# First layer by seven products, mixed with the second layer of the group before, and attention by whole chunks

## The chip, the cores and the metric

The kernel runs on one core of a Trainium2 chip. The metric is the time of one execution on the device in microseconds; the median over the runs is compared. Engines are named as in the profile: PE (TensorE; PEld are its weight loads), DVE (VectorE), ACT (ScalarE), POOL (GpSimd) and SP (SyncE, which here only issues DMAs).

## The reference

Two stages follow each other. The first is a linear attention with decay: 4 batches, 8 heads, 768 positions, 64 channels per head, computed in blocks with a state per head.

```python
intra = einsum('bhic,bhjc->bhij', qb, kb) * Dmask[None]      # lam ** (i - j), zero above the diagonal
intra = einsum('bhij,bhjd->bhid', intra, vb)
inter = einsum('bhid,bhde->bhie', qb * lam_pow[None], kv_state)
out[:, :, sl] = intra + inter
kv_state = lam_block * kv_state + einsum('bhsd,bhse->bhde', kb * rev_pow[None], vb)
```

Its result, as 3072 tokens of 512 numbers, goes through two dense layers: h = x @ w_in (512 to 2048), g = h * tanh(softplus(h)), out = g @ w_out (2048 to 512). Inputs and output are float32; the kernel computes in float16 with float32 sums.

## The kernel before, in words

Chunks have 128 positions; six groups n = 0 to 5 hold the four batches' chunks n, 512 tokens each. Per chunk the eight heads are four pairs of 64 + 64 channels. A dense first layer of a group (`mm1_unit`, L420) is 16 units of 4 matmuls with 512 columns, each followed by one Mish on ACT (L434). The second layer is plain for group 0 (`mm2_unit`, L442: 16 steps of 4 matmuls with 512 columns). For groups 1 to 5 it is Strassen's scheme in Winograd's form (`fast_unit`, L525): seven products of 2 x 8 matmuls with 256 columns, with sums of weights (`tsum`, L479) and of tokens (`gsum`, L498) made on DVE, and the results put together by `after`.

Attention works by half chunks (four heads). `att_a` scales q by its decay on DVE (`qT`, L318) and copies the scaled k into a zero-padded tile `kz` (L322); `att_s` makes scores from them with padded, full-height matmuls (L358) and masks them on DVE (`sb`, L362); `att_o` adds the state's part and the scores' part (L375, L379); the state is updated by `raw` on DVE (L298) and `w` on POOL (L299). k is scaled on POOL (`scale_k`, L259, on DVE for the first and last group). Group 0 has a form of its own, `first_t`, `first_s`, `first_o`: raw scores from half-height matmuls (L230), which are multiplied by a full table of decays `dm` (L234).

The order of work is written out by hand: each engine runs its instructions in the program's order. Group n's two layers run one after the other on PE, and the pieces of attention of group n + 1 are spread over them by a table (`room`). k, q and v come in chunk by chunk, 128 KB each in float16, by DMAs that POOL issues (L69, L77, L80); the weights come by POOL too (L93, L96, L103). Transposes of q and k from group 2 on are DMAs on SP. [...]

## Time and profile before

| what | value |
|---|---|
| median of 3 runs | 220.56 us (219.73 to 220.97) |
| profiled execution | span 217.4 us; the page gives no other time of it |
| median less that span | 3.2 us |
| granted clock of TensorE | 1.000 |
| loads by POOL's queue | 13.37 MB written, 78,080 packets |

The page gives busy time and share of the span for each engine; the chain of waits goes back from the last instruction to what released it at each step. In rows of the timeline the columns are start, length, engine, line, operation, tiles, count and, in brackets, how long the engine was idle before and what ended that. In the table by stage, behind each engine's busy time stands the number of its instructions, then the clock, the DMA engines' share and GB/s.

### The profile page before, as it was taken

How to read it: one execution, taken by the hardware profiler on the slowest of the kernel's cores; microseconds unless marked ns; L12 is line 12 of the kernel's file. 1: busy time of each engine (PE TensorE's matmuls, PEld its weight loads, DVE VectorE, ACT ScalarE, POOL GpSimd, SP SyncE). 2: the span in 40 equal slices, each digit the busy share in tenths (PEclk: the TensorE clock that was granted, in tenths of full speed). 3: DMA queues.
4: the chain of work that ended last, by engine and by line, in shares of the span. 5: the costliest groups of instructions: out<-in, count | busy, mean ns of one | idle time of the engine just before them, and what ended most of it. 6: DMA issues, size and time to landing. Idle time of an engine off the chain costs nothing.

```text
span 217.4 us, 4272 instructions
## 1 busy us (share of the span) xinstructions
PE 204.8 (94%) x1672; PEld 136.6 (63%) x1672; DVE 146.1 (67%) x309; ACT 101.3 (47%) x190; POOL 116.6 (54%) x139
## 2 busy tenths in 40 slices
PE   7899999999999799999979999979999999999993
PEld 2465544576545587745669845669845699644893
DVE  6667561877669999339999419999439987213433
ACT  5465566567665231166522176623166632266410
POOL 7996334998988768808757908757700002000020
PEclk9999999999999999999999999999999999999999
DMA  9999999999999999975999965999985201300014
...
DMA packets 103766, 24.66 MB, mean 113 GB/s; under 512 B 93890, under 2 KB 103234, under 8 KB 103746
## 3 DMA queue, kind: packets, MB, share of 16 engines
q0 software_dynamic: 78080, 13.37, 80.3%
...
q8 instruction: 13, 0.21, 0.4%
...
## 4 chain that ended last, share of the span: by engine, by line
PE 63%; DVE 20%; POOL 5%; issue 4%; DMA 4%; ACT 1%; ACTq 0%; POOLq 0%; DVEq 0%
PE ph L420 26%; PE z L525 10%; PE po L442 6%; PE y L525 6%; PE x L525 5%; DVE qT L318 5%; DVE kz L322 4%; DVE sb L362 4%; DVE gsum L498 4%; DMA win<-in_moe_w_in_dram 4%; PE pO L379 3%; DVE raw L298 3%; PE pS L358 2%; PE fin L525 2%; POOL vz L80 2%
## 5 line engine op out<-in xcount | busy, mean ns | idle before, releaser
L420 PE MATMUL ph<-xt,win 128*128 128x512 f16 (+2 forms) x404 | 89.6, 368 | 0.5 <-ACT hsg L434 0.2
L434 ACT ACTIVATE hsg<-ph 128x512 f16<-128x512 f32 x96 | 57.0, 597 | 45.6 <-PE ph L420 45.5
L420 PEld LDWEIGHTS <-win 128*128 128x128 f16 x404 | 37.0, 98 | 35.1 <-issue 0.6
L299 POOL TENSOR_TENSOR w<-raw,lbm 128x256 f16<-128x256 f32 x32 | 25.2, 791 | 29.0 <-DVE raw L298 28.9
L578 POOL TENSOR_TENSOR u<-u,p 128x512 f32<-128x512 f32 x5 | 6.5, 1293 | 52.0 <-DVE u L576 52.0
L525 PEld LDWEIGHTS <-gsum 128*128 128x128 f16 x336 | 30.8, 98 | 3.5 <-issue 0.5
L362 DVE TENSOR_TENSOR sb<-pS,maskT 128x512 f16<-128x512 f32 x40 | 27.2, 683 | 2.0 <-PE pS L358 1.9
L382 ACT ACTIVATE xt<-pO 128x256 f16<-128x256 f32 x40 | 15.2, 382 | 27.4 <-PE pO L379 27.2
L318 DVE TENSOR_TENSOR qT<-qraw,lq 128x256 f16<-128x256 f16 x32 | 19.1, 598 | 10.3 <-DMA qraw<-qn 10.3
L525 PEld LDWEIGHTS <-hsg 128*128 128x128 f16 x240 | 22.7, 98 | 2.5
L69 POOL DMA_DIRECT2D kn<-in_k_dram x23 | 21.4, 932 | 4.5 <-DMA win<-in_moe_w_in_dram 1.7
...
L498 DVE TENSOR_TENSOR gsum<-hsg 128x1024 f16<-128x1024 f16 x20 | 14.5, 725 | 12.9 <-ACT hsg L434 12.9
L322 DVE COPY kz<-kraw 64x256 f16<-64x256 f16 x64 | 19.9, 311 | 1.9 <-DMA kraw<-ktil 0.9
L379 PE MATMUL pO<-sb,vz 128*128 128x128 f16 x160 | 17.3, 219 | 3.6 <-DVE sb L362 3.2
L525 PE MATMUL z<-tsum,gsum 128*128 128x256 f16 x160 | 20.4, 272 | 0.2
L525 PE MATMUL x<-wout,hsg 128*128 128x256 f16 x160 | 20.1, 273 | 0.0
L358 PE MATMUL pS<-qT,kz 128*128 128x128 f16 x160 | 16.6, 220 | 1.8 <-DVE kz L322 1.6
L358 PEld LDWEIGHTS <-kz 128*128 128x128 f16 x160 | 11.8, 98 | 7.8 <-DVE kz L322 3.0
L298 DVE TENSOR_TENSOR raw<-pv,w 128x256 f32<-128x256 f32 x32 | 13.5, 422 | 4.1 <-PE pv L283 3.4
L379 PEld LDWEIGHTS <-vz 128*128 128x128 f16 x160 | 12.6, 98 | 5.7 <-issue 4.9
...
## 6 DMA issues: line engine op xcount, KB each, us to landing
...
win<-in_moe_w_in_dram POOLq DMA_DIRECT2D x3, 512.0 KB, 10.1
...
```

The costliest lines, as they stand in the source:

```text
L69: nc.gpsimd.dma_start(out=kn[i], in_=chunk_rows(k, i))
L80: nc.gpsimd.dma_start(out=vz[i % NVB][:, :, 0:D], in_=chunk_rows(v, i))
L299: nc.gpsimd.tensor_tensor(out=w_new, in0=raw, in1=lb, op=ALU.mult)
L318: nc.vector.tensor_tensor(out=s.qT, in0=qraw[i][:, 2 * hf : 2 * hf + 2, :], in1=lqh, op=ALU.mult)
L322: nc.vector.tensor_copy(s.kz[rs, :, hp, :], kraw[i][rs, 2 * hf : 2 * hf + 2, :])
L358: nc.tensor.matmul(psS[:, 2 * p + hp, :], s.kz[:, p, hp, :], s.qT[:, p, :], start=True, stop=True,)
L362: nc.vector.tensor_tensor(out=s.sb, in0=psS, in1=bc(maskT, 1, 4), op=ALU.mult)
L379: nc.tensor.matmul(psO[:, p, :], vf[:, o : o + 128], s.sb[:, 2 * p + hp, :], start=False, stop=(hp == 1))
L420: nc.tensor.matmul(ph_t[ni][:, lo:hi], win0[min(ni, 2)][:, kc, max(ni - 2, 0) * 128 : max(ni - 2, 0) * 128 + 128] if ni < w else win[ni // ...
L434: nc.scalar.activation(hsg[n][:, ni, :], ph_t.pop(ni), AF.Mish)
L498: nc.vector.tensor_tensor(out=gsum[n, i][:, ks, :], in0=a, in1=b, op=op)
L525: nc.tensor.matmul(t, lhs(kk, b), rhs(kk, c, c + w), start=(fresh and kk == 0 and (alone or i == 0)), stop=(kk == HK - 1), skip_group_chec ...
```

## The change

The first layer gets the same seven-product scheme as the second: a "set" is a quarter of its output rows (512 of 2048), seven products of 4 matmuls with 256 columns (`seven`, `set_step`), with sums of weights (`wsum`) and of tokens (`xsum`) from DVE. Groups 2 to 5 take it for all four sets, group 1 for two of them; group 0 keeps plain units. Group 0's second layer takes the seven products too (`dense2`). The loop over n now mixes three things, product by product: group n's second layer, group n + 1's first layer and group n + 2's attention (`quarter`: one set, three or four halves of second-layer products, one chunk). Group 1's attention stands among group 0's units. Attention runs by whole chunks in the form that group 0 had: raw scores from half-height matmuls in banks e and o, `dm` on DVE, and q decayed on the side for the state's part (`qd`). `kz`, its copies and the mask go. Loads are pairs of chunks (256 KB), and the first two groups' pairs stand between the weights' pieces. Each PSUM bank has one tag and one buffer: A, B, C for sets and units, G, H for the second layer, e, o, z for attention. `raw` has one buffer, the state's `w` one per batch.

```diff
+    def bank(tag, shape, dtype=F32):
+        return ps.tile([128] + shape, dtype, name=f"b{tag}", tag=f"b{tag}")
...
+    def load_pair(t, n, bp):
+        src, store = {"k": (k, kn), "q": (q, qn), "v": (v, vn)}[t]
+        if t == "v":
+            tile_ = vz[(2 * n + bp) % NVP]
+            nc.gpsimd.dma_start(out=tile_[:, :, 0:D], in_=rows(v, n, 2 * bp, 2))
+        else:
+            tile_ = loads.tile([128, 2 * H, D], F16, name=f"{t}n", tag=f"{t}n", bufs=4)
+            nc.gpsimd.dma_start(out=tile_, in_=rows(src, n, 2 * bp, 2))
+        pairs[t, n, bp] = tile_
+        for i in range(2):
+            store[n, 2 * bp + i] = tile_[:, i * H : (i + 1) * H, :]
...
+    load_win(0, 256, WQ)
+    load_win(1)
+    for t in "kqv":
+        load_pair(t, 1, 0)
+    load_win(2)
+    load_win(3)
+    for t in "kqv":
+        load_pair(t, 1, 1)
     for s in range(WS):
         load_wout(s)
...
+    def scores(n, b):
+        p_ = [bank(t, [JP, C]) for t in "eo"]
         for j in range(JP):
             for t in range(2):
                 rs = slice(64 * t, 64 * t + 64)
...
+                nc.tensor.matmul(p_[t][:, j, :], kT[n, b][rs, j, :], qT[n, b][rs, j, :],
+                                 start=True, stop=True)
         for t in range(2):
...
+            sb[n, b, t] = work.tile([128, JP, C], F16, name="sb", tag="sb", bufs=4)
+            nc.vector.tensor_tensor(out=sb[n, b, t], in0=p_[t], in1=dm[:, t], op=ALU.mult)
+    def outputs(n, b, tag="z"):
+        po = bank(tag, [JP, C])
+        vf = vn[n, b].rearrange("p h c -> p (h c)")
+        if n > 0:
+            for j in range(JP):
+                nc.tensor.matmul(po[:, j, :], wst[n, b][:, j, :], qd[n, b][:, j, :],
+                                 start=(j == 0), stop=False, skip_group_check=True)
         for j in range(JP):
             for t in range(2):
                 o = 4 * D * j + D * t
...
+                nc.tensor.matmul(po[:, j, :], vf[:, o : o + 128], sb[n, b, t][:, j, :],
+                                 start=(n == 0 and j == 0 and t == 0), stop=(t == 1),
+                                 skip_group_check=True)
+        nc.scalar.activation(x_tile(n)[:, :, b * C : (b + 1) * C], po, AF.Copy)
+    def state(n, b, tag="e"):
+        pv = bank(tag, [JP, 128])
+        for j in range(JP):
...
+                pv[:, j, :].rearrange("p (a e) -> p a e", a=2), flat(kd[n, b], j),
+                vn[n, b][:, 2 * j : 2 * j + 2, 0:D], start=True, stop=True)
+        w_new = const.tile([128, JP, 128], F16, name=f"w{b}") if n == 0 else wst[n, b]
         if n == 0:
...
+            nc.vector.tensor_tensor(out=w_new, in0=pv, in1=lbm, op=ALU.mult)
...
+            raw = work.tile([128, JP, 128], F32, name="raw", tag="raw", bufs=1)
+            nc.vector.tensor_tensor(out=raw, in0=pv, in1=wst[n, b], op=ALU.add)
+            nc.gpsimd.tensor_tensor(out=w_new, in0=raw, in1=lbm, op=ALU.mult)
+        wst[n + 1, b] = w_new
...
+    def w_sum(s, i, eng):
+        w, t = win[s], wsum[s]
+        a, b_, op = (
+            (w[:, 0:2, HC:], w[:, 2:4, HC:], ALU.add),
+            (t[:, 0], w[:, 0:2, 0:HC], ALU.subtract),
+            (w[:, 0:2, 0:HC], w[:, 0:2, HC:], ALU.subtract),
+            (w[:, 2:4, 0:HC], t[:, 1], ALU.subtract),
+        )[i]
+        eng.tensor_tensor(out=t[:, i], in0=a, in1=b_, op=op)
...
+    def x_sums(n):
+        x = xt[n]
+        t = [work.tile([128, 2, HC], F16, name=f"xsum{i}", tag=f"xsum{i}", bufs=1) for i in range(4)]
+        xsum[n] = t
+        for i, (a, b_) in enumerate((
+            (x[:, 0:2, HC:], x[:, 0:2, 0:HC]),
+            (x[:, 2:4, HC:], t[0]),
+            (x[:, 2:4, HC:], x[:, 0:2, HC:]),
+            (x[:, 2:4, 0:HC], t[1]),
+        )):
+            nc.vector.tensor_tensor(out=t[i], in0=a, in1=b_, op=ALU.subtract)
...
+    def seven(o, i, t, fresh):
+        w, x, ws, xs = win[o.s], xt[o.n], wsum[o.s], xsum[o.n]
+        for u in range(2):
+            for kk in range(2):
+                us = slice(u * 128, u * 128 + 128)
...
+                nc.tensor.matmul(t[:, u, :], lhs, rhs, start=(fresh and u == 0 and kk == 0),
+                                 stop=(kk == 1), skip_group_check=True)
...
+    def set_step(o, step):
+        if step == "m1":
+            o.a = bank("A", [2, HC])
+            seven(o, 1, o.a, True)
+            o.b = bank("B", [2, HC])
+            nc.scalar.activation(o.b, o.a, AF.Copy)
+        elif step == "m5":
+            o.c = bank("C", [2, HC])
+            seven(o, 5, o.c, True)
+            o.p5 = work.tile([128, 2, HC], F32, name="p5", tag="p5", bufs=1)
+            nc.scalar.activation(o.p5, o.c, AF.Copy)
+        elif step == "m2":
+            seven(o, 2, o.a, False)
+            mish(o, 0, 0, o.a)
+        elif step == "m6":
+            seven(o, 6, o.b, False)
+            nc.vector.tensor_tensor(out=o.c, in0=o.b, in1=o.p5, op=ALU.add)
+        elif step == "m7":
+            seven(o, 7, o.b, False)
+            c22 = work.tile([128, 2, HC], F32, name="c22", tag="c22", bufs=1)
+            nc.vector.tensor_tensor(out=c22, in0=o.b, in1=o.p5, op=ALU.add)
+            mish(o, 1, 1, c22)
+        elif step == "m3":
+            seven(o, 3, o.c, False)
+            mish(o, 0, 1, o.c)
+        elif step == "m4":
+            seven(o, 4, o.b, False)
+            mish(o, 1, 0, o.b)
...
+            if p == 1:
+                m.h = bank("H", [2, HN])
+                nc.scalar.activation(m.h, m.g, AF.Copy)
+            elif p == 2:
+                o = osum()
+                nc.scalar.activation(o, m.g, AF.Copy)
+                store(n, 0, 0, o)
+            elif p == 5:
+                m.p5 = work.tile([128, 2, HN], F32, name="r5", tag="r5", bufs=1)
+                nc.scalar.activation(m.p5, m.g, AF.Copy)
+                m.u4 = work.tile([128, 2, HN], F32, name="u4", tag="u4", bufs=1)
+                nc.vector.tensor_tensor(out=m.u4, in0=m.h, in1=m.p5, op=ALU.add)
+            elif p == 7:
+                o = osum()
+                nc.vector.tensor_tensor(out=o, in0=m.h, in1=m.p5, op=ALU.add)
+                store(n, 1, 1, o)
+            elif p == 3:
+                o = osum()
+                nc.vector.tensor_tensor(out=o, in0=m.g, in1=m.u4, op=ALU.add)
+                store(n, 0, 1, o)
...
+    state(0, 3, "o")
+    for i in range(2, NVP):
+        nc.vector.memset(vz[i][:, :, D : 2 * D], 0.0)
+    for bp in range(2):
+        for t in "kqv":
+            load_pair(t, 2, bp)
+    next_unit()
+    turn1(0)
+    next_unit()
+    decay_k(1, 0, nc.vector)
+    next_unit()
+    scores(1, 0)
+    turn1(1)
...
+    next_unit()
+    turn1(2)
+    next_unit()
+    decay_k(1, 2, nc.vector)
+    outputs(1, 1)
+    state(1, 1)
+    scores(1, 2)
...
+    next_unit()
+    w_sum(1, 0, nc.vector)
+    for ni, tag in ((0, "A"), (1, "B"), (2, "C")):
+        unit_part(1, ni, tag, 0, HC, True)
+    outputs(1, 3)
+    state(1, 3)
+    turn_dma(2, 0)
...
+    for part in range(2):
+        for i in (2, 0, 1, 3):
+            token_sum(0, i, part)
+    for ni in range(3):
+        unit_part(1, ni, "", HC, GT, False)
+        unit_end(1, ni)
+    unit(1, 3, "A")
+    for i in range(2):
+        weight_sum(0, i)
+        weight_sum(1, i)
+    for ni, tag in ((8, "B"), (9, "C"), (10, "A"), (11, "B")):
+        unit(1, ni, tag)
+    for i in range(2):
+        weight_sum(2, i)
+        weight_sum(3, i)
+    x_sums(1)
+    for i in range(1, 4):
+        w_sum(1, i, nc.vector)
...
+        set_step(o, "m1")
+        if att:
+            decay_q(m, b)
+        if n > 0:
+            if qi == 0:
                 token_sum(n, 0, 1)
                 token_sum(n, 1, 1)
...
+            elif qi == 1:
+                token_sum(n, 2, 1)
+                token_sum(n, 3, 1)
+        h()
+        if att:
+            scores(m, b)
+        set_step(o, "m5")
+        set_step(o, "m2")
+        set_step(o, "m6")
+        h()
+        if att:
+            outputs(m, b)
+            if m < NG - 1:
+                state(m, b)
+            if m + 1 < NG:
+                for t, bp in (("k", 0), ("q", 0)) if qi == 0 else (("v", 0), ("k", 1)) if qi == 1 else (
+                        ("q", 1), ("v", 1)) if qi == 2 else ():
+                    load_pair(t, m + 1, bp)
+        set_step(o, "m7")
+        set_step(o, "m3")
+        if qi == 2:
+            token_sum(n + 1, 0, 0)
+            token_sum(n + 1, 1, 0)
+        elif qi == 3:
+            token_sum(n + 1, 2, 0)
+            token_sum(n + 1, 3, 0)
+        h()
+        set_step(o, "m4")
+        while todo:
+            h()
...
+        for qi, nh in enumerate((4, 3, 4, 3)):
+            quarter(n, qi, halves, nh, ORDER[qi], n + 2 < NG)
+        if n + 2 < NG:
+            x_sums(n + 2)
```

The built program moves instructions at three places that matter below. The rows are in the order of the program, with what an instruction waits for; DMASW0 to 7 are the marks that POOL's loads set in turn, the one that a load waits for being the one that it will set itself, so it waits for the load eight places earlier. First POOL, in the opening, from the last of the weights to the first state updates (`w` with a number is the state of one batch). Before:

```order
L103 DMA wout_86<-in_moe_w_out_dram 128x4x512 [waits DMASW3_49]
L140 IOTA ei 128x128
L69 DMA kn<-in_k_dram 128x8x64 [waits DMASW4_49]
L77 DMA qn<-in_q_dram 128x8x64 [waits DMASW5_49]
...
L77 DMA qn<-in_q_dram 128x8x64 [waits DMASW6_49]
L80 DMA vz_76<-in_v_dram 128x8x64 [waits DMASW7_49]
L259 TENSOR_TENSOR ktil<-kn,lk 128x512 [waits Activation_49]
L299 TENSOR_TENSOR w_183<-raw,lbm 128x256 [waits DVE_49]
L299 TENSOR_TENSOR w_185<-raw,lbm 128x256 [waits DVE_49]
```

And now:

```order
L103 DMA wout_77<-in_moe_w_out_dram 128x4x512 [waits DMASW6_49]
L103 DMA wout_78<-in_moe_w_out_dram 128x4x512 [waits DMASW7_49]
L103 DMA wout_79<-in_moe_w_out_dram 128x4x512 [waits DMASW0_49]
L103 DMA wout_80<-in_moe_w_out_dram 128x4x512 [waits DMASW1_49]
L89 DMA kn<-in_k_dram 128x16x64 [waits DVE_49,DMASW2_49,PE_49,Activation_49]
L89 DMA qn<-in_q_dram 128x16x64 [waits DMASW3_49,PE_49]
L86 DMA vz_69<-in_v_dram 128x16x64 [waits DMASW4_49,PE_49]
L89 DMA kn<-in_k_dram 128x16x64 [waits DMASW5_49,DVE_49]
L89 DMA qn<-in_q_dram 128x16x64 [waits DMASW6_49]
L86 DMA vz_70<-in_v_dram 128x16x64 [waits DMASW7_49,PE_49]
L282 TENSOR_TENSOR w_388<-raw,lbm 128x512 [waits DVE_49]
L282 TENSOR_TENSOR w_403<-raw,lbm 128x512 [waits DVE_49]
```

Before, the loads ahead of the first `w` are group 1's twelve; now they are the weights and group 2's six pairs, and the last of these (v) waits for wout_78, the second piece of w_out.

Second DVE, where group 1's attention takes its second chunk (`sb` are the scores times decays, `raw` the state's sum). Before:

```order
L341 TENSOR_TENSOR qT<-pq,lq 128x256 [waits PE_49]
L298 TENSOR_TENSOR raw<-pv,w_188 128x256 [waits PE_49]
L362 TENSOR_TENSOR sb<-pS,maskT 128x512 [waits PE_49]
L341 TENSOR_TENSOR qT<-pq,lq 128x256 [waits PE_49]
L298 TENSOR_TENSOR raw<-pv,w_190 128x256 [waits PE_49,Pool_49]
L362 TENSOR_TENSOR sb<-pS,maskT 128x512 [waits PE_49]
```

And now:

```order
L281 TENSOR_TENSOR raw<-be,w_388 128x512 [waits PE_49]
L253 TENSOR_TENSOR sb<-be,dm 128x512 [waits PE_49]
L253 TENSOR_TENSOR sb<-bo,dm 128x512 [waits PE_49]
L227 COPY qT<-bz 128x512 [waits PE_49]
L238 TENSOR_TENSOR qd<-qT,lq 128x512 [waits DVE_49]
L242 TENSOR_TENSOR kd<-kn,lk 128x512 [waits DMASW3_49]
L281 TENSOR_TENSOR raw<-be,w_403 128x512 [waits PE_49,Pool_49]
L253 TENSOR_TENSOR sb<-be,dm 128x512 [waits PE_49]
```

The second `raw` waits for POOL, which has to read the first one out of the only buffer, and the scores of the next chunk write bank e, which this `raw` reads. Before, the first that waited so was the fourth `raw`, and its tag had two banks.

Third DVE again, where one group's turn ends and the next begins in the loop (`c` and `bC` are sums of a set, `gsum` token sums of the second layer, `xsum` those of the first):

```order
L281 TENSOR_TENSOR raw<-be,w_433 128x512 [waits PE_49,Pool_49]
L386 TENSOR_TENSOR c_1700<-bB,p_1654 128x512 [waits PE_49]
L431 TENSOR_TENSOR gsum_1708<-hsg 128x1024
L431 TENSOR_TENSOR gsum_1710<-hsg,gsum_1586 128x1024 [waits DVE_49]
L335 TENSOR_TENSOR xsum_1728<-xt 128x512 [waits Activation_49]
...
L335 TENSOR_TENSOR xsum_1731<-xt,xsum_1729 128x512 [waits DVE_49,PE_49]
L238 TENSOR_TENSOR qd<-qT,lq 128x512 [waits DMAHW1_49]
L431 TENSOR_TENSOR gsum_1584<-hsg 128x1024 [waits Activation_49]
L431 TENSOR_TENSOR gsum_1586<-gsum_1584,hsg 128x1024 [waits DVE_49]
L253 TENSOR_TENSOR sb<-be,dm 128x512 [waits PE_49]
L253 TENSOR_TENSOR sb<-bo,dm 128x512 [waits PE_49]
```

Before, at most two token sums stood next to each other, and there were no sums of the first layer's tokens; here eight sums and the decay of q stand between the last `raw` of one turn and the first `sb` of the next.

777 lines of the change are left out of this document (319 added, 458 removed).

## The prediction

> **What bounds the kernel now.** I read the page's busy times and the chain of waits first, then the table by stage, then single rows of the timeline.
>
> ```profile
> PE 204.8 (94%) x1672; PEld 136.6 (63%) x1672; DVE 146.1 (67%) x309; ACT 101.3 (47%) x190; POOL 116.6 (54%) x139
> PE 63%; DVE 20%; POOL 5%; issue 4%; DMA 4%; ACT 1%; ACTq 0%; POOLq 0%; DVEq 0%
> ```
>
> TensorE is busy for 94% of the span and holds 63% of the chain; VectorE holds 20% of it, though busy for only 67%. So there are stages in which VectorE decides. By stage (columns: length, busy time of PE, PEld, DVE, ACT, POOL):
>
> ```profile
> 57.00:90.60 33.60, 30.96 (x261) 21.68 (x261) 26.41 (x52) 13.22 (x26) 27.93 (x32) 1.00 1.49 115
> 90.60:124.00 33.40, 31.98 (x274) 22.65 (x272) 25.52 (x52) 14.21 (x27) 22.20 (x27) 1.00 1.05 112
> 157.40:188.00 30.60, 30.60 (x258) 21.67 (x256) 21.49 (x48) 14.17 (x27) 1.27 (x1) 1.00 0.36 76
> ```
>
> A middle group takes 33.4 us, 32.0 of them PE's, beside 25.5 of DVE. The group in which POOL has nothing to do takes 30.6 us without a gap. The prices of the work on PE stand in the chain (start, us, what):
>
> ```profile
> 90.65 6.04 PE ph L420 x28
> 114.07 0.22 PE pS L358 x4
> 120.56 1.75 PE z L525 x16
> 212.28 1.78 PE fin L525 x24
> 214.08 0.29 DVE osum L562
> ```
>
> A first-layer matmul of 512 columns costs 6.04/28 = 0.216 us, one of 256 columns 1.75/16 = 0.109, one of 128 columns 0.22/4 = 0.055. After the last product, at 214.06, come 3.3 us of tail.
>
> **The change on PE.** A set of the first layer by products is 28 matmuls of 256 columns, 3.06 us, for 16 of 512, 3.45. There are 18 sets (all four of groups 2 to 5, two of group 1): 18 x 0.39 = 7.0 us less. Group 0's second layer becomes 112 matmuls of 256 for 64 of 512: 12.25 for 13.80, 1.55 less. Raw scores are pairs on half the rows, a form that group 0 has already:
>
> ```profile
> 15.45 0.23 PEld L230 LDWEIGHTS <-pkT 64*128 64x128 f16 x8 [0.26 <-ACT pkT L218]
> 15.45 0.40 PE L230 MATMUL pS<-pqT,pkT 64*128 64x128 f16 x8
> ```
>
> Eight issue in about 0.23 us, where eight of the padded kind take 0.44: 20 chunks x 0.21 = 4.2 less. PE loses 12.7 us of work. A middle group is then 12.25 + 12.25 + 4 x (0.23 + 12 x 0.055 + 4 x 0.055) = 29.0 us; 28.1 in the loop that needs no state; 24.5 in the one without attention.
>
> **The opening: POOL's queue.** The built order lets a load be issued on POOL only when the load eight places earlier has landed. Rows of the timeline show it:
>
> ```profile
> 21.39 0.87 POOL L77 DMA_DIRECT2D qn<-in_q_dram  x1 [1.75 <-DMA win<-in_moe_w_in_dram]
> 36.60 0.87 POOL L77 DMA_DIRECT2D qn<-in_q_dram  x1 [1.68 <-DMA wout<-in_moe_w_out_dram]
> 37.18 0.69 DVE L259 TENSOR_TENSOR ktil<-kn,lk 128x512 f16<-128x512 f16 x1 [6.70 <-DMA kn<-in_k_dram]
> ```
>
> From the second quarter of win to the last of wout POOL was let on seven times, with six intervals in 15.2 us: one 512 KB load each 2.53 us. The next chunk (128 KB) landed 0.6 us later, so it too goes by bytes. This stall cost nothing before, since PE had all of mm1(0) and mm2(0) to do. Now the six pairs of group 2 stand on POOL ahead of the state's w<-raw (L282) of group 1, and `raw` has one buffer: raw(1,1) on DVE waits for w(1,0), and scores(1,2) on PE waits for raw(1,1), both being in bank e. The last pair goes out when wout1 has landed: 21.4 (win1) + six pairs of 256 KB + four loads of 512 KB (10.1). A pair is not in the trace: 1.27 us by bytes, 1.75 if two chunks go at POOL's issue spacing of 0.87; I take the bytes, as the row at 37.18 does. That makes 39.1 (to 42.0). The last issue takes 0.9 (up to 1.8, if it grows with the rows), w(1,0) 1.3 and raw 0.68, with prices from here:
>
> ```profile
> L578 POOL TENSOR_TENSOR u<-u,p 128x512 f32<-128x512 f32 x5 | 6.5, 1293 | 52.0 <-DVE u L576 52.0
> L362 DVE TENSOR_TENSOR sb<-pS,maskT 128x512 f16<-128x512 f32 x40 | 27.2, 683 | 2.0 <-PE pS L358 1.9
> L434 ACT ACTIVATE hsg<-ph 128x512 f16<-128x512 f32 x96 | 57.0, 597 | 45.6 <-PE ph L420 45.5
> ```
>
> So scores(1,2) starts at **42.5 us** (to 46). PE's own work up to it (units 4 to 12 and what stands between) would be done at 33.7: some 8.5 us idle. Part of this shows earlier, as unit 8 waits for win2, now queued behind three pairs (21.4 + 3.8 + 2.5 = 27.7, PE there at 25.5). What is left of PE's work from 42.5 on, without any further stall, ends at 200.5, with the tail 203.8.
>
> **VectorE's backlog.** DVE's prices back to back, and what POOL does to them:
>
> ```profile
> 54.52 2.49 DVE L479 TENSOR_TENSOR tsum<-wout,tsum 128x1024 f16<-128x1024 f16 x4
> 85.39 1.28 DVE L362 TENSOR_TENSOR sb<-pS,maskT 128x512 f16<-128x512 f32 x2
> 97.35 0.84 POOL L299 TENSOR_TENSOR w<-raw,lbm 128x256 f16<-128x256 f32 x1 [5.74 <-DVE raw L298]
> 97.52 1.76 DVE L322 COPY kz<-kraw 64x256 f16<-64x256 f16 x2
> 98.16 1.03 POOL L259 TENSOR_TENSOR ktil<-kn,lk 128x512 f16<-128x512 f16 x1
> 101.35 0.47 DVE L322 COPY kz<-kraw 64x256 f16<-64x256 f16 x2
> ```
>
> Each of the large kinds takes 0.60 more when one follows another. The two copies of kz need 0.47 us; at 97.52 they needed 1.76 and ended with POOL's second operation. A DVE operation on SBUF alone waits until POOL's pair of operations is through; one that reads PSUM (sb, raw) keeps 0.68 throughout. Of the new work, decay_q, the token, weight, w and x sums are of the first kind.
>
> From scores(1,2) the rest of att(1) is 7.5 us of PE with the wait for bank e, so raw(1,3) ends near 50.7. Then DVE has in a row eight token sums of group 0 and eight weight sums (16 x 0.60), POOL's w and decay_k between (2.35), and the first x sum (0.34): m5 of the first set can start at 63.0. PE has 8.0 us to do until there and stands for 4.5. The rest of this loop is DVE's: x and w sums 2.0, then 4 decay_q, 8 sb, 4 adds of the sets, 3 of the second layer, 4 token sums, 4 raw (27 x 0.60), 12 w sums (12 x 0.34), 20.3 in all, and some 3.5 of waits for POOL and for PE's results; the loop ends on PE at **87.5**. x and w sums have half a token sum's elements; at a full 0.60 each, 6 us more by the end.
>
> **The loops after it.** Per group DVE has 35 operations of 0.60 and 4 x sums: 22.4 us, against PE's 29.0. But w (1.3) and the next decay_k (1.05) now follow one another on POOL where group turns to group, so the token sums, the x sums and then sb come late: walked step by step, outputs of the first quarter waits 2.9 us for sb, and that of the third 0.35, since u4 stands on DVE ahead of sb. I take 32.2 for n = 2, 33.2 for n = 1 (it starts with the backlog), 29.6 for n = 3 (no decay_k, no raw), 25.2 for n = 4: 120.2, where PE alone has 110.6. ACT (some 32 operations of 0.6 per group, 19 us) has room. The last second layer is as before: 12.25 and 0.25 for its token sums.
>
> **Sum.** 87.5 + 120.2 + 12.5 + 3.3 = 223.5 us of span, against 217.4: 12.7 us of PE's work go and, by the same count, some 9.7 of its old stalls, and 28.5 of new ones come (8.8 before 42.5, the rest behind it: 223.5 - 203.8). The page gives its execution's span alone; the median of the runs, 220.56, lies 3.2 above it. So **226.7 us**, 2.8% slower.
>
> **The rivals.**
> *PE stays the bound.* The stop at 42.5 is there, but afterwards DVE is late only as often as before (33.4 less 13.80 + 12.25 + 5.3 of PE's own is 2 us a loop, four loops): 203.8 + 8 + 3.2 = 215. For it speaks that DVE has only 22.4 of 29.0; against it that it had 25.5 of 33.4 before, and that the backlog's 12 us stand in one row with 8 of PE. Chance 0.22. It ends faster.
> *Backlog without blocking.* All as forecast up to 87.5, then loops with 1 us, 1, 0.4 and 0.2 of stall, because POOL's operations happen to fall beside DVE's reads of PSUM: 87.5 + 113.2 + 12.5 + 3.3 + 3.2 = 219.7, about level. Chance 0.12.
> *PE restarts slowly.* Two idle stretches of over 4 us are new; the longest in the table of waits (us in all, times, longest) was 1.2. At the start PE was slow:
>
> ```profile
> PE pO L379 <- DVE sb L362: 3.2, 4, 1.2
> ...
> 9.17 0.63 PE L162 MATMUL busy<-kzero 128*128 128x512 f16 x1
> 12.12 0.38 PE L162 MATMUL busy<-kzero 128*128 128x512 f16 x1
> ```
>
> If each of the two is followed by 4 us at that rate, nearly half of them are lost, twice 1.7 us: 226.7 + 3.4 = 230, and with slow pairs (42.0 for 39.1) 233. Against it: after the first stop DVE decides anyway and hides part. Chance 0.17. [...]
> *The change doesn't do what it says*: products of 256 columns cost more than 0.109 beside attention. The rows of z and x at 1.75 for 16 stand in such a mix already; no chance of its own.
>
> **How the numbers follow.** The forecast (222 to 229) has 0.47, the first rival 0.22, the level case 0.12, the slow restart 0.17; 0.02 for the rest. Half a per cent, about 1.1 us, is what a measurement here can tell from none. Faster: 0.22 and a quarter of the level case's, 0.25. Same 0.07, slower 0.68. The range, 213 to 234, reaches over the first rival's sum and over slow pairs with a slow restart; the forecast's own is 222 to 229.
>
> **What would show it.** Right: PE idle from about 34 until 42 to 46 with raw(1,1) waiting for POOL, the load of v just before w on POOL; a wait of m5 for the x sums near 60; loops of 32 to 33 us with waits of outputs for sb in every first quarter. Wrong: PE above 95% between 45 and 90, or loops of 30. The PE rows should show 0.44 us per product of a set and 0.23 per chunk of scores; otherwise PE's part of the sum is wrong.

## The result and the profile after

The changed kernel takes 240.99 us in the median (239.37 to 241.25), the kernel before 220.76 in the same comparison: 1.089 times as long, with a 95% interval of 1.082 to 1.096. I had forecast 226.7, and 213 to 234 as the range. The sign was right; the size was about a third of what came.

First the page of the changed kernel: busy times, clock by slices, chain of waits, and VectorE's largest group.

```profile
PE 202.0 (84%) x1936; PEld 160.1 (67%) x1936; DVE 170.9 (71%) x278; ACT 109.8 (46%) x196; POOL 89.1 (37%) x86
PEclk9998999679997999999999999999999999999999
PE 44%; DVE 27%; DMA 13%; POOL 9%; issue 5%; ACT 1%; DVEq 0%; POOLq 0%
L431 DVE TENSOR_TENSOR gsum<-hsg 128x1024 f16<-128x1024 f16 x24 | 22.6, 951 | 0.0
```

TensorE's share of the chain fell from 63% to 44%. It is nearly as long busy as before (202.0 after 204.8), although it has fewer columns to compute. Part of that is the clock, as busy time is longer where it is low: the row of PEclk (slices of 6 us) shows it low from 18 to 24 us (0.81 granted), from 42 to 54 (0.68, then 0.75) and from 72 to 78 (0.76). DMA and GpSimd, at 4% and 5% before, now hold 22%.

The table by stage (length; busy PE, PEld, DVE, ACT, POOL; clock; DMA), cut at the starts of the loops on TensorE:

```profile
98.83:133.12 34.29, 30.81 (x325) 26.33 (x321) 30.33 (x41) 16.05 (x30) 17.73 (x15) 1.00 1.15 117
133.12:166.27 33.15, 30.48 (x322) 26.20 (x320) 29.19 (x40) 17.55 (x34) 16.73 (x15) 1.00 1.09 112
166.27:197.17 30.90, 29.45 (x307) 25.32 (x304) 21.93 (x37) 17.92 (x34) 0.14 (x1) 1.00 0.19 53
197.17:222.75 25.58, 25.38 (x227) 21.90 (x225) 13.90 (x24) 15.30 (x29) 0.00 (x0) 1.00 0.12 43
222.75:239.40 16.65, 12.43 (x130) 11.16 (x127) 6.24 (x13) 3.06 (x6) 1.27 (x1) 0.98 0.24 80
```

The four loops take 34.3, 33.2, 30.9 and 25.6 us, where I had 33.2, 32.2, 29.6 and 25.2. The loop of n = 1 starts at 98.8, where I had 87.5. So most of the miss lies ahead of 98.8. There the timeline of TensorE shows the two stops:

```profile
46.95 0.26 PE L249 MATMUL be<-qT,kT 64*128 64x128 f16 x1 [5.36 <-DVE raw L281]
47.49 1.89 PE L298 MATMUL bB<-xt,win 128*128 128x512 f16 x4
50.02 1.49 PE L298 MATMUL bC<-xt,win 128*128 128x512 f16 x4
53.59 1.04 PE L298 MATMUL bA<-xt,win 128*128 128x512 f16 x4
71.03 0.67 PE L359 MATMUL bC<-xsum,wsum 128*128 128x256 f16 x4 [4.59 <-DVE xsum L335]
73.33 1.78 PE L468 MATMUL bG<-wout,hsg 128*128 128x256 f16 x8
75.84 1.04 PE L468 MATMUL bG<-wout,hsg 128*128 128x256 f16 x8
```

Each stop is followed by rows of nearly double length (1.89 for 1.04; 1.78 for 1.04); the granted clock is 0.50 from 46.9 to 49 us and 1.00 from 53.6 to 55. The first stop is GpSimd's: it holds the queue for two loads before it comes to w.

```profile
39.92 1.14 POOL L89 DMA_DIRECT2D qn<-in_q_dram  x1 [1.01 <-DMA wout<-in_moe_w_out_dram]
43.73 1.14 POOL L86 DMA_DIRECT2D vz<-in_v_dram  x1 [2.68 <-DMA wout<-in_moe_w_out_dram]
44.89 1.27 POOL L282 TENSOR_TENSOR w<-raw,lbm 128x512 f16<-128x512 f32 x1
```

Two things I had not seen at all. In the opening VectorE stands 2.2 us for `ei`, a ramp that GpSimd makes behind loads (L129), since `q_decays` now comes early, and ScalarE stands for VectorE; and at the end the last part of the output stands for a buffer. From the timelines of ScalarE and of VectorE:

```profile
13.28 0.63 ACT L571 ACTIVATE lq<-lq 128x512 f32<-128x512 f32 x1 [2.49 <-DVE lq L190]
236.43 0.29 DVE L551 TENSOR_TENSOR osum<-bC,c 128x128 f32<-128x128 f32 x1 [1.34 <-DMA out_dram<-osum]
```

### The profile page after: what moved, and what is told of

Its sections match the earlier page's. It is cut to its first block, busy times and chain, and to the rows that moved or that the text cites. A ratio compares the mean times of both kernels' runs of the same rounds, so it can differ in the third digit from the quotient of the medians.

```text
span 239.4 us, 4700 instructions
## 1 busy us (share of the span) xinstructions
PE 202.0 (84%) x1936; PEld 160.1 (67%) x1936; DVE 170.9 (71%) x278; ACT 109.8 (46%) x196; POOL 89.1 (37%) x86
## 4 chain that ended last, share of the span: by engine, by line
PE 44%; DVE 27%; DMA 13%; POOL 9%; issue 5%; ACT 1%; DVEq 0%; POOLq 0%
PE bG L468 10%; PE bH L468 9%; DVE gsum L431 7%; DMA wout<-in_moe_w_out_dram 7%; PE bB L359 7%; PE bC L359 5%; DMA qn<-in_q_dram 4%; PE bA L359 4%; DVE sb L253 4%; DVE xsum L335 3%; PE bz L265 3%; DVE raw L281 2%; DVE qd L238 2%; DVE wsum L321 2%; DVE tsum L412 2%
## 5 line engine op out<-in xcount | busy, mean ns | idle before, releaser
L282 POOL TENSOR_TENSOR w<-raw,lbm 128x512 f16<-128x512 f32 x16 | 22.0, 1372 | 64.7 <-DVE raw L281 64.6
L468 PEld LDWEIGHTS <-gsum 128*128 128x128 f16 x400 | 37.9, 98 | 5.6 <-issue 1.4
L359 PEld LDWEIGHTS <-wsum 128*128 128x128 f16 x288 | 26.5, 98 | 11.6 <-issue 6.0
L468 PE MATMUL bH<-tsum,gsum 128*128 128x256 f16 x192 | 24.6, 273 | 1.1 <-DVE u L496 1.0
L468 PE MATMUL bG<-wout,hsg 128*128 128x256 f16 x192 | 25.3, 278 | 0.0
L268 ACT ACTIVATE xt<-bz 128x512 f16<-128x512 f32 x20 | 11.9, 597 | 27.7 <-PE bz L265 27.5
L359 PEld LDWEIGHTS <-win 128*128 128x128 f16 x216 | 21.3, 99 | 3.7 <-issue 1.2
L253 DVE TENSOR_TENSOR sb<-be,dm 128x512 f16<-128x512 f32 x24 | 16.5, 686 | 8.9 <-PE bo L249 8.9
L359 PE MATMUL bB<-xsum,wsum 128*128 128x256 f16 x144 | 22.0, 276 | 0.5 <-DVE xsum L335 0.4
L363 ACT ACTIVATE hsg<-c 128x512 f16<-128x512 f32 x18 | 11.3, 630 | 23.7 <-DVE c L386 23.7
L359 PE MATMUL bA<-xt,win 128*128 128x256 f16 x144 | 22.1, 277 | 0.0
L281 DVE TENSOR_TENSOR raw<-be,w 128x512 f32<-128x512 f32 x16 | 11.0, 690 | 14.6 <-PE be L273 10.1
L249 PE MATMUL be<-qT,kT 64*128 64x128 f16 x96 | 9.8, 224 | 11.6 <-DVE raw L281 7.2
L238 DVE TENSOR_TENSOR qd<-qT,lq 128x512 f16<-128x512 f16 x20 | 17.9, 896 | 0.2
L265 PE MATMUL bz<-sb,vz 128*128 128x128 f16 x160 | 13.0, 219 | 5.8 <-DVE sb L253 5.6
L249 PEld LDWEIGHTS <-kT 64*128 64x128 f16 x192 | 6.2, 96 | 17.3 <-issue 11.6
```

What stands on the lines that cost most here:

```text
L238: nc.vector.tensor_tensor(out=qd[n, b], in0=qT[n, b], in1=lq, op=ALU.mult)
L249: nc.tensor.matmul(p_[t][:, j, :], kT[n, b][rs, j, :], qT[n, b][rs, j, :], start=True, stop=True)
L253: nc.vector.tensor_tensor(out=sb[n, b, t], in0=p_[t], in1=dm[:, t], op=ALU.mult)
L265: nc.tensor.matmul(po[:, j, :], vf[:, o : o + 128], sb[n, b, t][:, j, :], start=(n == 0 and j == 0 and t == 0), stop=(t == 1), skip_group_ ...
L268: nc.scalar.activation(x_tile(n)[:, :, b * C : (b + 1) * C], po, AF.Copy)
L281: nc.vector.tensor_tensor(out=raw, in0=pv, in1=wst[n, b], op=ALU.add)
```

## The experiments

Each kernel is compared with the kernel before in runs on the same chip; a number like 1.069 is the ratio of times, with its 95% interval. The experiments ran on several chips, so two of them are compared by these ratios; times within a run are read from its profiled execution. The theory at the start: the 20 us come from late rows in the opening (gate, clock, `ei`), from VectorE standing for GpSimd, and from the loops that this makes. The rival: TensorE is the bound and the products simply cost more than they save.

**The opening.** Four kernels, each an edit of the changed kernel. `e1_gate` moves two of the six loads behind group 1's last state; `e2_iota` moves the ramp; `e3_both` does both; `e4_warm` leaves everything and gives TensorE something to do in the stop.

```diff
 e1, e3
-    for bp in range(2):
-        for t in "kqv":
-            load_pair(t, 2, bp)
+    for t, bp in (("k", 0), ("q", 0), ("v", 0), ("k", 1)):
+        load_pair(t, 2, bp)
...
     state(1, 3)
+    for t in "qv":
+        load_pair(t, 2, 1)
 e2, e3: iota(ei, ...) from behind load_win(0, 128, 256) to directly behind iota(ek, ...)
 e4
     state(1, 1)
+    busy(24)
     scores(1, 2)
```

> The loads of q and v of group 2's second pair are issued behind the last state of group 1, the other four stay; nothing else differs from the changed kernel. Theory (the gate sets the start of VectorE's backlog): w(1,0) no longer stands behind a load that waits for wout, scores(1,2) starts near 42 instead of 46.95, the matmuls behind it run at full rate (first-layer row 1.03 us for four instead of 1.89), the first token sum starts near 51.5 instead of 58.5, and all 7 us reach the end: 234 us. Rival 1 (the weights' landing sets the backlog): VectorE starts earlier but stands for wout in the weight sums, 239 to 241. Rival 2 (the gate is only the stop, the clock plays no part): 5 us, 236.

> Only the ramp ei is moved on GpSimd, from behind the first two quarters of win to directly behind ek. Theory: VectorE's lq no longer stands 2.2 us and ScalarE's exponential 2.5 us, the first unit of the first layer starts near 17 instead of 21.2, but wout's landing still sets scores(1,2) near 47, so the end stays: 240 to 242 us, and TensorE's stop before scores(1,2) grows from 5.4 to 9 or 10 us. Rival (the opening's loss goes through to the end): 236 us.

> Both edits together: the ramp ei early, and two of the six loads behind group 1's last state. Theory: now the opening's 4 to 5 us count, as no load of wout stands ahead of w(1,0); the fourth pair's load still holds GpSimd until about 39, so a stop of some 3 us stays: scores(1,2) near 39 to 40, first token sum near 48.5, 231 us (9 to 10 less than the changed kernel). Rival (the two edits do not add, VectorE's sums are bound by wout or by something else): no better than the moved loads alone, 234 or more.

> 24 matmuls of zeros by zeros (512 columns, 5.2 us) are put into TensorE's stop ahead of scores(1,2); the gate stays. Theory (TensorE is slow after the stop): the first-layer rows behind the gate take 1.03 us for four instead of 1.89 and 1.49, the first token sum starts some 2 us earlier, 239 us. Rival (the rate after the stop decides nothing, VectorE and GpSimd set the pace from there): rows as fast, but 240.5 to 241.5 us.

Measured: e1 236.36 us, 1.069 (1.064 to 1.075); e2 239.96, 1.087 (1.079 to 1.096); e3 235.25, 1.064 (1.059 to 1.069); e4 240.12, 1.086 (1.080 to 1.092). From the timelines of TensorE, one row each of e2, e3 and e4:

```profile
46.06 0.26 PE L249 MATMUL be<-qT,kT 64*128 64x128 f16 x1 [7.67 <-DVE raw L281]
```

```profile
63.32 1.01 PE L359 MATMUL bC<-xsum,wsum 128*128 128x256 f16 x4 [5.44 <-DVE xsum L335]
```

```profile
46.07 1.04 PE L298 MATMUL bB<-xt,win 128*128 128x512 f16 x4
```

In e2 the first unit starts at 17.2 instead of 21.2, but scores(1,2) still starts at 46.1: the stop has merely grown to 7.7 us. What `ei` costs, 4 us at that point, is hidden behind the landing of wout. Not all of these 4 us are the ramp: e1 leaves it where it was and starts the first unit at 19.6, because its rows behind the stop at 16.4 run at full rate (eight matmuls on sb in 0.62 us) and those of the changed kernel do not (0.95 us). e2 and e4 differ too little from the changed kernel in time (1.087 and 1.086 for 1.089) to be told apart from it.

With the gate moved, the first token sum starts at 51.4 (e1) and 49.8 (e3) instead of 58.4, so the opening gains 7.0 and 8.6 us, yet only 4.6 and 5.7 reach the end. Both came out where their rivals had them, e1 by the number only, since its rows behind the gate run at full rate (1.04 us for four matmuls of 512 columns). The second stop does not shrink (5.4 us in e3): VectorE's row of sums is its cause, wherever it starts. In e4 the rows behind the gate run at full rate (1.04 us, the last row above), and the first token sum starts 3.1 us earlier. Of these, 1.2 us are not the clock: scores(1,2) started at 45.7 in this execution, for which I take an earlier landing of wout. From there to the token sum 9.6 us pass instead of 11.4, so the clock is worth 1.9 us at that place. The profiled execution ends 1.5 us earlier. One place where the rest goes, in e3 and by the length of that loop in e4 too, shows in the timeline of e3: at the turn to the loop of n = 1, where TensorE waits 1.55 and 0.38 us for sb, the clock falls once more.

```profile
98.43 0.22 PE L265 MATMUL bz<-sb,vz 128*128 128x128 f16 x1 [1.55 <-DVE sb L253]
99.03 0.55 PE L265 MATMUL bz<-sb,vz 128*128 128x128 f16 x7 [0.38 <-DVE sb L253]
100.74 1.91 PE L468 MATMUL bG<-wout,hsg 128*128 128x256 f16 x8
```

In the changed kernel the same waits stand there and the rows behind them keep 0.87 us for eight; so its loop of n = 1 is 1.3 to 1.7 us shorter than that of e1, e3 and e4 (36.3 against 37.6 to 38.0 on TensorE, from one end of product 4 to the next). In e3 another 0.85 us go in the loop of n = 0, which takes 38.7 us from the first token sum on instead of 37.85; with the 1.7 this is all that separates the 8.6 us of the opening from the 6.0 by which its span is shorter. Fixing the opening moved the place where the clock falls.

**VectorE, GpSimd and the products.** From e3: `e5_plain` brings back the plain first layer, `e6_early` moves VectorE's sums forward, `e7_nopool` leaves GpSimd's work out (state and keys are not decayed from group 2 on, so its result is another one), `e8_ahead` was to part GpSimd's two operations.

```diff
 e5: in set_step, a plain unit at four of the seven steps; x_sums and w_sum are not called
+        at = ("m1", "m5", "m7", "m3") if o.n == 1 else ("m1", "m5", "m2", "m7")
+        if step in at:
+            unit(o.n, 4 * o.s + at.index(step), "CAB"[spin[0] % 3])
+            spin[0] += 1
+        return
 e6: behind decay_k(1, 2) and behind w_sum(1, 0)
+    for i in (2, 0):  # and (1, 3)
+        token_sum(0, i, 0)
     x_sums(1) and w_sum(1, 1..3) ahead of the weight sums
 e7
+            if n > 1:
+                nc.vector.tensor_tensor(out=w_new, in0=pv, in1=wst[n, b], op=ALU.add)
     decay_k: if n > 1, kd[n, b] = kn[n, b]
 e8: decay_k(m, b + 1) ahead of state(m, b), instead of decay_k(m, b) at the quarter's start
```

> From the kernel with both early edits (235.3 us): the first layer of groups 1 to 5 by plain units of 512 columns again, at the places of the products; x sums, w sums and the sets' additions fall away. Theory (VectorE, stretched by GpSimd, sets the pace from the backlog on): TensorE gets 7 us more work, VectorE some 36 us less (12 additions of 0.60 in groups 1's sets and the like, 0.60 x 8 and 1.4 per later group, 16 w sums of 0.34), the loops fall from 34, 33, 31, 26 to about 31.5, 31, 30, 26.3 and the loop of n = 0 loses 6: 224 us. Rival (TensorE is the bound, what stands is noise): its 7 us are added, 242 us.

> From the kernel with both early edits (235.3 us): group 0's four token sums of the first half go into VectorE's two gaps of the opening (1.8 and 2.5 us long), and the x sums and win1's sums stand ahead of the weight sums. Theory (VectorE has no gap from the token sums to the end of the loop of n = 0, so work taken out of that row counts in full): the wait of m5 for the x sums falls from 5.4 to under 1, the loop's end comes 4 to 6 earlier: 230 us. Rival (the row has room in it, behind it something else decides): 234 or more.

> From the kernel with both early edits (235.3 us). GpSimd's two operations of each chunk are left out from group 2 on: the state is not decayed and keys are not decayed (raw is written into w directly; the state uses the keys as loaded). VectorE has the same number of operations. Theory (VectorE's SBUF operations stand while GpSimd works, some 3 to 4 us in each of three loops and that of n = 0): the token sums fall from a mean of 0.95 to 0.70 us, qd from 0.90 to 0.65, loops of 30 instead of 34, 33 and 31: 223 us. Rival (the loops are held by the sets' own chain, product to addition to product, and by the second layer's): rows shorter, but loops over 32, 231 or more.

> From the kernel with both early edits (235.3 us): GpSimd's decay of the keys of the next chunk is issued ahead of the state of this one, so that w and the decay no longer follow one another without a gap where one group turns into the next. Theory (a VectorE operation stands through two GpSimd operations in a row, so parting them helps): about 1 us in each of four loops, 232 us. Rival (the total time of GpSimd counts, not its grouping; parted, it stops VectorE twice): 235 to 237.

Measured: e5 227.9 us, 1.036 (1.028 to 1.043); e6 236.1, 1.070 (1.063 to 1.078); e7 224.6, 1.020 (1.013 to 1.027); e8 237.0, 1.075 (1.066 to 1.083).

e5 settles the rival: with 7 us more work for TensorE by the count of columns, and VectorE busy for 134.7 us instead of 172.7, the kernel is 7.4 us faster (2.8% by the ratios). e7 settles GpSimd. The largest group of token sums in e3 and in e7, from the groups by line:

```profile
L431 DVE TENSOR_TENSOR gsum<-hsg 128x1024 f16<-128x1024 f16 x24 | 23.4, 985 | 0.0
L437 DVE TENSOR_TENSOR gsum<-hsg 128x1024 f16<-128x1024 f16 x24 | 17.2, 728 | 0.0
```

Measured on TensorE from one end of product 4 to the next, its loops take 32.9, 30.7, 30.1 and 25.3 us, those of e3 38.0, 33.2, 30.9 and 25.6. The loops of n = 1 and 2, which have GpSimd's work, lose 5.1 and 2.4; that of n = 0, from the first token sum on, 2.4 (36.3 for 38.7); those of n = 3 and 4, which have none, 0.8 and 0.2. Against it stand 2 us in e7's opening, where the clock fell (last section). So 9.9 of the 10.9 us gained in the loops come from those with GpSimd's work (the two profiled spans differ by 9.0); in that of n = 1 some 1.5 are the clock, which does not fall there in e7 (eight products in a row of 1.04 us at 97.4, against 1.91 in e3). Without GpSimd's work the token sums take 728 ns for 985 in the mean, qd 684 for 896 and the x sums 418 for 500, all of them from SBUF to SBUF; sb, which reads PSUM, takes 687 in both. e8 did not help, and it shows nothing on grouping: in the program the decay stands ahead of the state, but on GpSimd it still follows the state before without a gap, as in e3. From the timeline of GpSimd in e8, where one group turns into the next:

```profile
129.94 1.27 POOL L282 TENSOR_TENSOR w<-raw,lbm 128x512 f16<-128x512 f32 x1 [4.06 <-DVE raw L281]
131.16 1.49 POOL L242 TENSOR_TENSOR kd<-kn,lk 128x512 f16<-128x512 f16 x1
```

VectorE's time in gsum and qd is 60.4 us in place of 60.9. Whether parting the two would help was not tested.

e6 shows why VectorE's gaps were no room. The gap at 37.7 was the one in which GpSimd does w(1,0). From the timelines of VectorE, GpSimd and TensorE of e6:

```profile
37.92 3.00 DVE L431 TENSOR_TENSOR gsum<-hsg 128x1024 f16<-128x1024 f16 x2
```

```profile
38.49 1.27 POOL L282 TENSOR_TENSOR w<-raw,lbm 128x512 f16<-128x512 f32 x1
```

```profile
41.58 0.21 PE L249 MATMUL be<-qT,kT 64*128 64x128 f16 x1 [3.61 <-DVE raw L281]
```

Two sums that take 1.28 us in a row in e12 took 3.0, raw came 1.3 us later, TensorE stood 3.6 us instead of 2.6, and the clock fell behind it (four matmuls of 512 columns in rows of 1.53 and 1.85 us, 1.04 and 1.03 in e3).

**Clearing the opening.** `e9_plain_open` and its twin with products `e10_seven_open`:

```diff
     state(1, 1)
+    load_pair("k", 2, 1)
     scores(1, 2)
 (likewise q behind state(1, 2), v behind state(1, 3))
     scores(1, 3) ...
+    for i in (2, 0, 1, 3):
+        token_sum(0, i, 0)
 (weight_sum(2, .) and (3, .) behind the state of the loop's first quarter; osum bufs=3 -> 4)
```

> From the kernel with plain units in the first layer (227.9 us): the three loads of group 2's second pair are issued one behind each of the states (1,1), (1,2), (1,3); the four token sums of group 0's first half stand in VectorE's idle stretch behind scores(1,3), in which GpSimd has nothing to do; the last four weight sums stand behind the state of the loop's first quarter; four buffers for osum instead of three. Theory (three stops are left: 2.6 us before scores(1,2), 3.4 us before the second layer, some 3 us of slow clock behind them, and 1.3 us at the tail for a buffer): all go, 218 us, less than before. Rival (another wait takes their place, as when the token sums were put early): 224 to 227.

> The same edits of the opening and of the tail, with the first layer by seven products as in the changed kernel, and the x sums and win1's sums ahead of the weight sums (from the kernel with both early edits, 235.3 us). Theory (the loops and VectorE's row stay, only the stops and the slow clock go): 2.6 + 2 to 3 of the 5.4 us stop + 1.3 at the tail, 228 to 230 us, some 10 above its twin with plain units. Rival (once the opening runs, products are worth their 7 us of TensorE): as fast as the twin or faster, 218 or less.

Measured: e9 227.1 us, 1.028 (1.023 to 1.033); e10 237.1, 1.070 (1.063 to 1.076). e9 came out where its rival had it. e10 fits neither of its two: it is 10 us above its twin, as the theory had it, but gained nothing on e3 (1.064). The stop before scores(1,2) shrank to 1.8 us (e9) and 1.6 (e10), and the one behind VectorE's row went; in its place stands one that I had not had on the list, from the timelines of TensorE and of SyncE in e9:

```profile
61.65 0.26 PE L249 MATMUL be<-qT,kT 64*128 64x128 f16 x1 [4.17 <-DMA qT<-qn]
```

```profile
51.03 4.07 SPq L232 DMA_TRANSPOSE qT<-qn  x1
```

scores(2,0) waits for the transposed queries of group 2, which land 10.5 us after their issue (4.0 is the median of this run's sixteen transposes). The DMA engines are busy until then; in the table by stage of e9 the three last columns are clock, DMA share and GB/s:

```profile
58.00:62.00 4.00, 0.35 (x8) 0.38 (x8) 0.46 (x1) 0.10 (x1) 0.00 (x0) 0.81 2.17 162
62.00:66.00 4.00, 4.00 (x22) 2.22 (x17) 1.52 (x3) 0.60 (x1) 0.00 (x0) 0.50 0.20 36
```

So with these loads in this order group 2's attention begins at about 61 us, and TensorE needs other work up to then; that it is the loads that hold the transposes is read from these rows and was not tested by itself. `e11_fill` gives it: units 12 to 15 of group 1 go ahead of the second layer, and the weight sums back in front. `e12_act` takes GpSimd's tensor operations out of the loops and keeps the result.

```diff
 e12, in decay_k for n > 1
+            for h in range(H):
+                nc.scalar.activation(kd[n, b][:, h, :], kn[n, b][:, h, :], AF.Copy, scale=lk[:, h : h + 1])
 in state
-            nc.gpsimd.tensor_tensor(out=w_new, in0=raw, in1=lbm, op=ALU.mult)
+            (nc.vector if n > 1 else nc.gpsimd).tensor_tensor(out=w_new, in0=raw, in1=lbm, op=ALU.mult)
```

> From the last kernel with plain units (227.1 us), where scores(2,0) stood 4.2 us for the DMA transpose of group 2's queries: units 12 to 15 of group 1 (3.46 us of TensorE) are done ahead of the second layer of group 0 and no longer in the loop's second half, and the last four weight sums go back in front of the loop. Theory (group 2's data come when all loads ahead of them have landed, near 61 us, and TensorE only has to have work until then): the stop falls under 1 us, no slow clock behind it, the loop of n = 0 ends 3 to 5 us earlier, 223 us. Rival (VectorE and GpSimd set the loop's end whatever TensorE does in front): 226 to 227.

> On top of that, GpSimd has no tensor operation from group 2 on, with the result kept: the decay of the keys is done by ScalarE (8 activations of 64 columns per chunk), the state's by VectorE (16 operations more in all from group 2 on, less those of the last groups: 12 x 0.60 = 7.2 us of VectorE). Theory (standing through GpSimd's operations costs VectorE more than doing one of them itself): the loops of n = 0, 1 and 2 lose 2 us, 2 and 1, 218 us. Rival (ScalarE's row of short activations delays the copies that TensorE waits for): 223 or more.

Measured: e11 222.1 us, 1.009 (1.005 to 1.013): the theory's 5 us came. e12 221.8, 1.005 (1.002 to 1.008): not told apart from e11. Of the 4 us that I had expected of it little is left, because eight short activations take 2.0 us on ScalarE, and the second layer's copy r waits behind them. From its timeline of TensorE:

```profile
74.35 1.86 PE L481 MATMUL bH<-tsum,gsum 128*128 128x256 f16 x8 [2.69 <-DVE u L509]
```

**Do the products pay at all?** `e14_plain_late` issues that decay behind the scores; `e13_seven_late` has besides the products in groups 3 to 5. `e15_seven_gp` has the products in groups 3 to 5 with GpSimd's work (its twin is e11). `e16_two` has them in groups 4 and 5 only; `e17_turn` is e13 with another order of VectorE where group turns into group.

```diff
 e13, e15: in set_step
+        if o.n < 3 and step in at and (o.n, o.s) != (1, 3):
             unit(...)
+        if o.n < 3:
+            return
 e16: o.n < 4
 e17: x_sums(n + 2) ahead of the token sums of the fourth quarter;
      token_sum(n, 0, 1) and (n, 1, 1) behind scores instead of ahead
```

> From the kernel without GpSimd's operations (221.8 us): the keys' decay on ScalarE is issued behind the scores of its quarter, so that the second layer's copy r no longer stands behind it (a 2.7 us stop), and groups 3, 4 and 5 take the first layer by seven products again, with the 16 w sums spread over the loop of n = 1. Theory (products cost time only where VectorE is full or stands for GpSimd; with room on VectorE their 0.39 us a set reach the end): 3 us from the stop and its slow clock, 1.5 each in the loops of n = 2 and 3 and 0.7 in that of n = 4, 216 to 217.5 us, less than the kernel before. Rival (products cost more than they save wherever attention is mixed in): no better than the twin without them.

> The twin of that kernel with plain units throughout. Theory: only the stop goes, 218.5 to 219.5 us, 2 or more above the twin with products. Rival: as fast as the twin or faster.

> The products in groups 3, 4 and 5 as in the other kernel, but with GpSimd's decays of keys and state back (from the kernel with the filled opening, 222.1 us, which is its twin with plain units). Theory (products and GpSimd's blocking do not go together): the loop of n = 2 is 1 us or more longer than with plain units, that of n = 1 longer for its w sums, n = 4 half a us shorter, 223 to 224 us. Rival (the products lost only through the opening and the loop of n = 0): 219 to 220.

> From the kernel with plain units throughout and no operation of GpSimd in the loops (220.0 us): products in the first layer of groups 4 and 5 alone, whose loops (n = 3 and 4) measured 29.95 and 25.34 with products and 30.46 and 26.07 without; the 16 w sums are spread over the loops of n = 1 and 2. Theory (products pay where VectorE does no state): 1.2 us less, 218.8 us, faster than the kernel before by 0.7 to 0.9%. Rival (the sums at the turn from n = 2 to n = 3 eat the gain): 220 or more.

> From the kernel with products in groups 3, 4 and 5 and no operation of GpSimd in the loops (223.4 us): only VectorE's order where group turns into group: x sums ahead of the two token sums of the quarter, and the two token sums of the next quarter behind sb instead of ahead of it. Theory (the loop of n = 2 took 35.5 us because m5 and outputs wait behind a row of VectorE's operations at the turn): the waits of 1.1 and 1.5 us go, that loop comes to 32 to 33, 220 to 221 us. Rival (the loop is held by the number of VectorE's operations, not by their order): 223 to 224.

Measured: e13 223.4 us, 1.012 (1.007 to 1.016); e14 220.0, 0.996 (0.993 to 0.999); e15 227.9, 1.031 (1.027 to 1.036); e16 220.5, 1.001 (0.998 to 1.004); e17 223.0, 1.013 (1.008 to 1.017). e14 is the only one below the kernel before, by 0.4%, which is inside what I had called no change. It keeps the mixing, the whole chunks and the paired loads, and gives up the products in the first layer.

The products lost in every pair: 5.8 us with GpSimd's work (e15 to e11, 2.2% by the ratios), 3.4 without it (e13 to e14, on one chip). The loops tell where, cut on TensorE at the first matmul of a loop. That of n = 2 takes 35.1 us with products and 31.4 without; those of n = 3 and 4 take 30.3 and 25.3 against 30.5 and 26.1. The 29.95 for n = 3 that stands in what I expected of e16 was taken between ScalarE's copies of product 4; in e13 the copy at the end of the loop of n = 2 stood 1.3 us behind two Mish operations, which made that loop look longer and the next one shorter. So the products gain clearly only in the last loop (0.7 us), which has no attention; they are level in that of n = 3, which has attention but no state (0.1 us less in e13, 0.4 more in e3 than in e5), and lose 3.7 in that of n = 2, where VectorE also has the state. The loop of n = 1, in which e13 makes the w sums, loses 0.5. From the timeline of TensorE in e13, at the turn into the loop of n = 2:

```profile
117.77 0.60 PE L365 MATMUL bC<-xsum,wsum 128*128 128x256 f16 x4 [1.14 <-DVE xsum L341]
121.43 0.22 PE L270 MATMUL bz<-sb,vz 128*128 128x128 f16 x1 [1.10 <-DVE sb L258]
122.03 0.55 PE L270 MATMUL bz<-sb,vz 128*128 128x128 f16 x7 [0.38 <-DVE sb L258]
124.91 0.60 PE L365 MATMUL bB<-xsum,win 128*128 128x256 f16 x4 [0.36 <-DVE c L400]
```

TensorE's holes (from the start of one matmul to the next, less its price) add up to 6.2 us in this loop, to 0.9 in e14's. e17 reordered the row: the wait for the x sums went, one of 1.2 us for the set's own addition (bC) came, and the holes still add up to 5.8. So this other order did not help, which speaks for the number of operations on VectorE there. e16 gained the 0.7 us of the last loop and lost 0.9 in the loop of n = 3, where the products then begin: it shows no gain.

## Why the prediction was right or wrong

The span came out 15.9 us over the forecast (239.4 for 223.5): 11.3 up to the loop of n = 1, 3.7 in the loops, 1.0 at the tail. The 11.3 are 4.4 up to scores(1,2), 3.2 from there to the first token sum, 0.3 from there to m5 and 3.3 to the loop's end. The 3.2 us taken over for the time outside the span were wrong as well: in every run whose span is on record, of any of these kernels, it is 1.7 to 1.95 us. So the span of 217.4 belongs to an execution of some 219.2 us (an estimate from these), faster than the median that I set it against. By luck that error hid 1.6 us of the miss.

*PE's prices.* The products were right: 0.87 us for eight, 0.44 for four. The step on the scores was wrong: "eight issue in about 0.23 us", so 4.2 us less. The rows around them, in the timeline of the changed kernel and, for the padded kind, of the kernel before:

```profile
110.85 1.04 PE L468 MATMUL bH<-tsum,gsum 128*128 128x256 f16 x8
111.81 0.23 PE L249 MATMUL be<-qT,kT 64*128 64x128 f16 x1
112.14 0.61 PE L359 MATMUL bC<-xsum,wsum 128*128 128x256 f16 x4
```

```profile
113.91 0.39 PE L358 MATMUL pS<-qT,kz 128*128 128x128 f16 x4
114.13 0.22 PE L375 MATMUL pO<-qT,w 128*128 128x128 f16 x1
```

Eight products take 0.87, so the row at 110.85 is through at 111.72; the next full-height matmul starts at 112.14. A chunk of half-height scores thus takes 0.42 us of TensorE, with 0.09 ahead of it and 0.1 behind in which nothing issues, against 2 x 0.22 padded. Of the 4.2 us some 0.4 were there. The row that I quoted for group 0 stood at 15.45, and the one behind it at 15.99: I read the instruction's own length and not the distance to the next. This is 0.8 us in each of the loops of n = 1 to 3, 2.4 of the 3.3 that they are longer, if all of it lies on the path, which was not tested. Why nothing issues in the two holes was not shown.

*The opening: POOL's queue.* The mechanism is there row by row: the load that waits for the one eight places earlier, w behind v, raw behind w, scores(1,2) behind raw. The size was wrong: 46.95 for 42.5, just outside the bound of 46. The step that failed is "I take the bytes". From the landing of win1 (22.4, itself 1.0 later than taken) to that of wout1 (43.7) it took 21.3 us; four loads at 2.53 and six pairs at 1.27 make 17.7, at the 1.75 of my upper bound 20.6. By the times at which POOL was let on, the pairs landed 1.5 to 1.85 us apart, 9.7 us in all for 7.6, near the upper bound and not by their bytes; why is open. The other 1.5 us are the four weight loads, 11.6 us for 10.1, the last of which took 3.8. "Unit 8 waits for win2" did not show, because TensorE came later; in e7 and e8, where it comes earlier, unit 8 waits 0.4 and 1.2 us for win. The step that I had left out, `q_decays` moved in front of GpSimd's ramp, cost 4 us at the first unit. Its worth at the end, behind this gate, cannot be told from none: e2's span is 1.2 us shorter, and by as much its first token sum is earlier, behind scores(1,2), which came 0.9 us earlier, and 1.2 earlier in e4 too, with the ramp in its old place. The stop was 5.4 us instead of 8.5 because TensorE was through with its earlier work at 41.6 and not at 33.7; 3.2 of these 7.9 us go with the ramp (e2: 38.4), the rest has not been taken apart.

*PE restarts slowly.* I had this as a rival of 0.17 and left it out of the sum; its 4 us at the slow rate behind each stop, 1.7 us lost, were my estimate. Both stops were followed by slow rows; between scores(1,2) and the first token sum 11.4 us passed instead of 8.2, and the first four steps behind the second stop took 3.9 instead of 2.2. With the clock kept up by zeros (e4) it is 9.6 instead of 11.4, so the clock has 1.9 of the first 3.2 us and 1.7 behind the second stop; the other 1.3 us of the 3.2 were too little in my walk. My argument against it, that VectorE decides anyway and hides part, is not what happened: from the first token sum to the end of the loop of n = 0 both kernels take 37.85 us, so nothing is hidden there. Of the 1.9 us e4 lost 1.6 again in the loop of n = 1 (37.9 us for 36.3), by my estimate to the clock, as e3 did.

*VectorE's backlog.* Right: 12.6 us from the first token sum to the start of m5 (58.4 to 71.0), forecast 12.3 (50.7 to 63.0); stop 4.6, forecast 4.5. The rest of that loop took 27.8 us for 24.5. About half of the difference is the clock; 1.3 us are a slip in my own sum, as the 2.0, 20.3 and 3.5 us that I listed for it make 25.8 and not 24.5.

*The loops.* 34.3, 33.2, 30.9, 25.6 against 33.2, 32.2, 29.6, 25.2: right in kind (outputs of the first quarter wait for sb, 1.7 and 0.5 us of hole) and 0.4 to 1.3 short each, most of it the scores if these lie on the path. That blocking by GpSimd makes a large part of them is shown by e7; a wait of 1.0 us for sb stands in the changed kernel's loop of n = 3 too, in which GpSimd has nothing to do. The rival without blocking was wrong.

*PE stays the bound.* Wrong, and further from it than I gave: even with GpSimd out of the way, its state's work on VectorE, the products did not pay (e13 to e14).

*Tail.* 4.3 us for 3.3: the last output stood 1.3 us for one of three osum buffers.

So the forecast named the right chain and most of the right places, and was short in sizes that all went one way: the queue, with win1's later landing, 4.4 us, the clock 3.6, the scores up to 2.4, the rest of the first loop with the slip in the sum, the tail 1.0. Two of them, pairs and clock, had a higher bound or a rival in the text, and the sum took the lower one both times; the scores and the tail were given no bound at all.

Where the 20 us went, by the steps undone one after another (ratios to the kernel before): 1.089 as changed; 1.064 with the gate and the ramp moved; 1.036 with the plain first layer; 1.028 and 1.009 with the opening rearranged and filled; 0.996 without GpSimd in the loops, the keys' decay done by ScalarE behind the scores and the state's by VectorE. What stays open: whether the products would pay with the state's decay on an engine that is neither VectorE nor GpSimd. With that decay left out (e7) the loops of n = 2 to 4 were 1.7 us shorter in all than e14's; a kernel that keeps the result and has it so was not tried.
